# An attention and FFN kernel on one core: all engines in a written order up to the middle of the second FFN group, masks and rescale chains at places of their own, three more filler matmuls

## The chip, the cores and the metric

The kernel runs on one core of a Trainium2 chip. The metric is the device time of one execution in microseconds; the times given are medians over several executions of the same program. A core has five engines with an instruction queue each: TensorE (PE in the profile, its weight loads PEld), VectorE (DVE), ScalarE (ACT), GpSimd (POOL) and SyncE (SP). Each works through its own queue in order. An instruction can wait for semaphores that other engines or DMA transfers raise; everything behind it on the same engine then waits too.

## The reference

Sliding-window attention with four sink tokens feeds a gated FFN:

```python
keep = is_sink | in_window                     # window 128, first 4 tokens always kept
a = softmax(where(keep, q @ k.T / sqrt(64), -1e9))
x = (a @ v)                                    # (4, 8, 768, 64) -> (3072, 512)
xn = x / sqrt(mean(x * x) + 1e-6) * rms_g
out = (silu(xn @ w_gate) * (xn @ w_val)) @ w_out
```

q, k and v are 4 batches x 8 heads x 768 tokens x 64; w_gate and w_val are 512 x 1536, w_out is 1536 x 512. Inputs and output are float32. The kernel works in bfloat16 with float32 accumulation.

## The kernel before

The 3072 tokens are 24 blocks of 128 (`g` = 0 to 23, 6 a batch). Block `g` goes through these units:

- `unit_load` (L126): POOL issues three DMAs, q, k and v of the block (L108, L121), converted to bfloat16 on the way.
- `unit_t` and `unit_t1` (L284, L265): q and k are transposed on TensorE (L260) into PSUM (`pqk`) and copied to `qkT` by DVE or ACT (L298, L274). From block 12 on SP does it by DMA (L290).
- `unit_s` (L431): scores of the block's keys against the queries of the block and of the next one (L443, `pT`), exponential on ACT (L452, `et`), and the masks. `mask` (L411) takes DVE, one multiplication for all heads of a half (L418), for blocks below `POOL_MASK_FROM` and for the first block of a batch, and otherwise two `affine_select` for each half on POOL (L420, L425).
- `unit_attend` (L511): sink part (L476) and values (L490, L494) into `pv`; DVE divides by the sums (L526 `rden`, L531 `x`); ACT sums the squares (L548 `sq`).
- `unit_rms` (L560), the rescale chain: some six tiny DVE instructions (L565 to L593, `m` and `y`) find one over the root; `unit_xr` (L600) multiplies the block by it and by the gain (L611, `xr`).
- `unit_x` (L631): `xr` is transposed on TensorE (L638, `pxt`) and copied to `xnt` (L650, L652); from block 12 on by DMA.
- Four blocks make one FFN group (`G` = 0 to 5). `parts_f` (L671): gate matmuls (L664, `pg`), tanh on ACT (L682, `th`), value matmuls (L664, `pvl`), and two products on DVE (L687 `p`, L697 `hT`). `parts_o` (L741): output matmuls (L748, `po`), eviction on ACT (L755, `osb`), store by SP (L759).

All PSUM tiles come from one pool of eight banks, so a TensorE instruction that opens a tile also waits until ACT or DVE has read the tile that held its bank before.

`run` (L783) writes the order: it walks over the FFN parts of a group and puts the attention units of later blocks between them, each at the part number given beside it in a list. For some engines this order is binding (`manual_schedule`); on the others a planner orders the instructions by its own estimates. Before, all five engines are bound in the opening (L797) and in `byhand` (L851), the first half of group 0. From `first` on (L901) only TensorE, SP and POOL are bound; DVE and ACT are left to the planner. There the masks of a block are issued together with its scores, the chain of blocks 5, 6 and 7 hangs on the end of `unit_av` (L506), and the sink tiles of batch 1 (`unit_sink`, L334) are held behind a tanh. `unit_warm` (L355) multiplies a tile of zeros and nobody reads the result; the opening has six of these matmuls at its start and one later on.

The stretch around the change: blocks 4 to 7 are attended while group 0 ends and group 1 begins. Group 1 works in two column halves, of which the second, from part 12 on, is the one that needs blocks 6 and 7.

Of the kernel before, what the change touches and what calls it, by code (L numbers as in the profile page):

```python
# [28 lines left out]
def kernel(  # L29
# [26 lines left out]
    GB = 4  # L56
# [10 lines left out]
    DMA_X_FROM = 12  # L67
    LD = 15
    FA = FTN
    POOL_MASK_FROM = 8  # L70
    MANUAL = {mybir.EngineType.PE, mybir.EngineType.SP, mybir.EngineType.Pool}
    MANUAL_ALL = MANUAL | {mybir.EngineType.Activation, mybir.EngineType.DVE}

# [258 lines left out]
        VSK[b] = vs  # L332

    def unit_sink(b):  # L334
        with tc.issue_after(LAST_TANH[0]):
            unit_sink_k(b)
            unit_sink_v(b)
# [93 lines left out]
    def unit_s(g):  # L431

        b, t = divmod(g, NT)
        nq = 2 if t + 1 < NT else 1
        w = nq * P
        per = 512 // w
        nb = HP // per
        banks = [[bank() for hi in range(2)] for u in range(nb)]
        for hp in range(HP):
            u, j = divmod(hp, per)  # L440
            for hi in range(2):
                pr = slice(hi * D, (hi + 1) * D)
                nc.tensor.matmul(  # L443
                    out=banks[u][hi][:, j * w:(j + 1) * w],
                    lhsT=QKT[b][pr, 1, hp, t * P:(t + 1) * P],
                    rhs=QKT[b][pr, 0, hp, t * P:t * P + w],
                    start=True, stop=True,
                )
        for u in range(nb):
            et = epool.tile([P, 2, per, nq, P], BF16, name="et")  # L450
            for hi in range(2):
                nc.scalar.activation(  # L452
                    out=et[:, hi].rearrange("p j n c -> p (j n c)"), in_=banks[u][hi],
                    func=ACT.Exp, scale=inv_sqrt_d,
                )

            def masked(u, et, his):
                for hi in his:
                    for j in range(per):
                        for n in range(nq):  # L460
                            E[(g, 2 * (u * per + j) + hi, n)] = et[:, hi, j, n, :]
                e = et if len(his) == 2 else et[:, his[0]:his[0] + 1]
                mask(e.rearrange("p i j n c -> p (i j) n c"), g, nq)

            for his in [(0, 1)] if nq == 2 else [(0,), (1,)]:
                masked(u, et, his)

    PVB = {}

    def unit_sink_av(g):  # L470
        b, t = divmod(g, NT)
# [10 lines left out]
    def unit_av(g, u):  # L482
        b, t = divmod(g, NT)

        pv = PVB.pop((g, u)) if t >= 2 else psum.tile(
            [P, 512], FP32, name="pv", tag="b1")
        for i, h in enumerate(range(H)[heads_of(g, u)]):
            dest = pv[:, i * VW:(i + 1) * VW]
            if t >= 1:
                nc.tensor.matmul(  # L490
                    out=dest, lhsT=E[(g - 1, h, 1)], rhs=V16[b][:, t - 1, h, :],
                    start=(t == 1), stop=False, skip_group_check=True,
                )
            nc.tensor.matmul(  # L494
                out=dest, lhsT=E[(g, h, 0)], rhs=V16[b][:, t, h, :],
                start=(t == 0), stop=True, skip_group_check=True,
            )
        if u == 0:
            X16[g] = xpool.tile([P, H, D], BF16, name="x16", bufs=7)
        pvv = pv[:, 0:HW].rearrange("p (h c) -> p h c", c=VW)  # L500
        if g < 2:
            PV[(g, u)] = pvv
        else:
            unit_norm(g, u, pvv)
            unit_sq(g, u)
        if u == 1 and g in (5, 6, 7):  # L506
            unit_rms(GROUP[g])
            for i in GROUP[g]:
                unit_xr(i)

    def unit_attend(g):  # L511

# [87 lines left out]
    def unit_xr(g):  # L600
        y = Y.pop(g)
        x16 = X16.pop(g).rearrange("p h d -> p (h d)")
        xr = xpool.tile([P, DM], BF16, name="xr", bufs=4)
        if g == 1:
            nc.scalar.mul(xr, x16, y)
        elif g == 0:
            nc.vector.tensor_scalar(
                out=xr, in0=x16, scalar1=y, scalar2=None, op0=ALU.mult,
            )
        else:  # L610
            nc.vector.scalar_tensor_tensor(  # L611
                out=xr, in0=x16, scalar=y, in1=gb, op0=ALU.mult, op1=ALU.mult,
            )
        G, tb = divmod(g, GB)
        if tb == 0:
            XNT[G] = xtpool.tile([P, KTN, GN], BF16, name="xnt")
        if g >= DMA_X_FROM:
            nc.sync.dma_start_transpose(  # L618
                out=XNT[G][:, :, tb * P:(tb + 1) * P], in_=xr,
            )  # L620
        else:
            XR[g] = xr
# [155 lines left out]
                slots[4].append(lambda n=n: unit_t(n))  # L778
        return [(p + i, u) for i, us in enumerate(slots) for u in us]

    AT = [(10, 16, 20, 24, 30), (0, 10, 18, 27)]

    def run(parts, slots):  # L783

# [12 lines left out]
    with tc.manual_schedule(engines=MANUAL_ALL):  # L797
# [8 lines left out]
        unit_t1(1, 0)  # L806
        unit_sp(0, 0)
        unit_t1(1, 1)
        unit_sp(0, 1)
        unit_sp(1, 0)  # L810
        unit_sink_k(0)
        unit_attend01(0, 0)
        unit_attend01(0, 1)
# [29 lines left out]
    def fa(ft, **kw):  # L843
        return parts_f(0, (ft, ft + 1), h0, **kw)
# [1 line left out]
    def fq(cols, ft):  # L846
        return parts_f(0, tuple(range(ft, ft + 4)), cols)

    byhand = (fa(0, split=True, between=lambda: (unit_rms((2,)), unit_xr(2))) + fa(2) + fa(4) + fq(b2, 0) + fa(6) + fq(b2, 4) + fa(8))
    first = fa(10) + fq(b3, 0) + fq(b3, 4) + fq(b2, 8) + fq(b3, 8)  # L850
    with tc.manual_schedule(engines=MANUAL_ALL):  # L851
        run(byhand, [
            (1, lambda: unit_sink_v(0)),
            (1, lambda: unit_sink_scores(0, 2, 1)),
            (2, lambda: unit_attend(2)),
            (7, lambda: unit_x(2)),
            (7, lambda: unit_t1(3, 0)),
            (7, lambda: unit_bias(2, 1)),
            (8, lambda: unit_t1(3, 1)),
            (9, lambda: unit_sink_scores(0, 3, 1)),  # L860
            (9, lambda: unit_sp(2, 1)),
            (9, lambda: unit_bias(3, 0)),
            (9, lambda: unit_sp(3, 0)),
            (11, lambda: unit_attend(3)),
            (12, lambda: (unit_rms((3,)), unit_xr(3))),
        ])
    FIRST = [
        (2, lambda: unit_x(3)),
        (1, lambda: unit_t1(4, 0)),
        (1, lambda: unit_bias(3, 1)),  # L870
        (2, lambda: unit_t1(4, 1)),
        (2, lambda: unit_sp(3, 1)),
        (2, lambda: unit_t1(5, 0)),
        (4, lambda: unit_sink_scores(0, 4)),
        (4, lambda: unit_s(4)),
        (5, lambda: unit_t1(5, 1)),
        (6, lambda: unit_s(5)),
        (7, lambda: unit_t(6)),
        (8, lambda: unit_attend(4)),
        (10, lambda: unit_attend(5)),  # L880
        (16, lambda: unit_t(7)),
        (16, lambda: unit_sink(1)),
        (18, lambda: unit_s(6)),
        (18, lambda: unit_x(4)),
        (19, lambda: unit_x(5)),
        (19, lambda: unit_t(8)),
        (21, lambda: unit_attend(6)),
        (22, lambda: unit_s(7)),
        (24, lambda: unit_t(12)),
        (24, lambda: unit_t(13)),  # L890
# [2 lines left out]
        (0, lambda: unit_t(9)),  # L893
        (4, lambda: unit_attend(7)),
        (4, lambda: unit_x(6)),
        (6, lambda: unit_sink_scores(1, 2)),
        (6, lambda: unit_s(8)),
        (7, lambda: unit_t(10)),
        (9, lambda: unit_x(7)),
    ]  # L900
    with tc.manual_schedule(engines=MANUAL):  # L901

        for g in range(2 * GB + 2, 2 * GB + 6):
            FIRST.append((3 * g - 30, lambda g=g: unit_load(g)))
        for G in range(NG):
            if G == 0:
                parts, slots = first, FIRST
            else:
                parts, slots = [], []
                for cols in (h0, h1) if G == 1 else (slice(0, GN),):  # L910
                    n = GN // (cols.stop - cols.start)
                    for ft in range(0, FTN, n):
                        parts += parts_f(G, tuple(range(ft, ft + n)), cols)
                g0, n = (9, 5) if G == 1 else (4 * G + 6, 4)
                for g in range(g0, min(g0 + n, NB + 1)):
                    slots += step(g, AT[G > 1][g - g0])
                if G == 1:
                    slots += SECOND
                    for g, p in enumerate((0, 0, 7, 11, 17, 21, 25, 27, 31, 33), 14):
                        slots.append((p + 0.5, lambda g=g: unit_load(g)))  # L920
                if G + 2 <= NG:
                    gs = GROUP[GB * (G + 1)]
                    slots.append((25, lambda gs=gs: unit_scale(gs)))
                    for i, g in enumerate(gs):
                        slots.append((30 + i, lambda g=g: unit_x(g)))
            for tb in range(GB):
                parts += (parts_last if G * GB + tb == NB - 1 else parts_o)(G, tb)
            run(parts, slots)
# [1 line left out]
_INS = ['q', 'k', 'v', 'n_sink', 'window', 'moe_w_gate', 'moe_w_val', 'moe_w_out', 'moe_rms_g']  # L930
_OUTS = [((3072, 512), 'float32')]
# [30 lines left out]
```

## Time and profile before

| | |
|---|---|
| median of 7 runs | 249.03 us (248.65 to 250.43) |
| the profiled execution | 248.56 us, of which its span 246.9 us |
| TensorE busy | 238.8 us, 97% of the span |
| DVE busy | 165.4 us, 67% |
| ACT busy | 137.9 us, 56% |
| POOL busy | 104.2 us, 42% |
| granted TensorE clock | 1.00 of full in the profiled execution |

The span runs from the first to the last instruction of the program. Busy shares are means over stages with different limits. A row of a timeline gives start and duration in us, engine, line, operation, what is written and read, how many instructions of a kind follow each other, and in brackets how long the engine had been idle and who ended that. A row of the waits reads: who waited for whom, us in total, how often, the longest. Matmuls are pipelined, so a row's duration is longer than the distance to the next one's start.

### The profile page before, as it was taken

How to read it: one execution, taken by the hardware profiler on the slowest of the kernel's cores; microseconds unless marked ns; L12 is line 12 of the kernel's file. 1: busy time of each engine (PE TensorE's matmuls, PEld its weight loads, DVE VectorE, ACT ScalarE, POOL GpSimd, SP SyncE). 2: the span in 40 equal slices, each digit the busy share in tenths (PEclk: the TensorE clock that was granted, in tenths of full speed). 3: DMA queues.
4: the chain of work that ended last, by engine and by line, in shares of the span. 5: the costliest groups of instructions: out<-in, count | busy, mean ns of one | idle time of the engine just before them, and what ended most of it. 6: DMA issues, size and time to landing. Idle time of an engine off the chain costs nothing.

```text
span 246.9 us, 5312 instructions
## 1 busy us (share of the span) xinstructions
PE 238.8 (97%) x2022; PEld 138.2 (56%) x2041; DVE 165.4 (67%) x379; ACT 137.9 (56%) x323; POOL 104.2 (42%) x141
## 2 busy tenths in 40 slices
PE   8999999999979999999999999999999999999995
PEld 3668788756867884554454444444444444344443
DVE  5648788756998688349778278769168885097700
ACT  3795669446566875975583385674465242323212
POOL 8976677498868598871232001233131000000000
PEclk9999999999999999999999999999999999999999
DMA  9999999999999999999001665001610004710012
GB/s 129 144 183 179 193 157 207 166 176 187 203 149 135 72 84 141 160 187 158 0 0 24 169 170 69 1 0 25 191 42 3 0 0 45 171 42 0 1 73 101
DMA packets 104940, 25.52 MB, mean 103 GB/s; under 512 B 94033, under 2 KB 101969, under 8 KB 104914
## 3 DMA queue, kind: packets, MB, share of 16 engines
q0 software_dynamic: 80704, 13.90, 77.6%
q1 hardware_dynamic: 23026, 10.95, 20.4%
q10 hardware_dynamic: 1184, 0.33, 0.6%
q8 instruction: 16, 0.26, 0.4%
q14 instruction: 10, 0.08, 0.1%
HBM read 28.31 MB, written 6.29 MB: 140 GB/s over the span
## 4 chain that ended last, share of the span: by engine, by line
PE 83%; DVE 12%; issue 1%; SPq 1%; DMA 1%; ACT 1%; DVEq 0%; ACTq 0%
PE pg L664 23%; PE pvl L664 22%; PE po L748 19%; PE pT L443 3%; PE pv L490 3%; PE pv L494 2%; DVE xr L611 2%; PE pqk L260 2%; DVE p L687 2%; DVE hT L697 2%; PE pT L370 1%; SPq L618 1%; PE pw L359 1%; DVE x L531 1%; PE po L730 1%
## 5 line engine op out<-in xcount | busy, mean ns | idle before, releaser
L664 PE MATMUL pg<-xnt,wg 128*128 128x512 bf16 (+2 forms) x431 | 74.0, 304 | 1.4 <-DMA xnt<-xr 0.5
L664 PE MATMUL pvl<-xnt,wv 128*128 128x512 bf16 (+2 forms) x438 | 74.2, 305 | 0.1
L687 DVE SCALAR_TENSOR_TENSOR p<-th,pg 128x512 bf16<-128x512 bf16 x72 | 49.1, 684 | 27.8 <-ACT th L682 27.7
L682 ACT ACTIVATE th<-pg 128x512 bf16<-128x512 f32 x72 | 43.0, 601 | 38.6 <-PE pg L664 37.0
L748 PE MATMUL po<-wo,hT 128*128 128x512 bf16 x268 | 61.4, 379 | 0.4
L697 DVE TENSOR_TENSOR hT<-p,pvl 128x512 bf16<-128x512 bf16 x72 | 49.4, 687 | 7.6 <-DVE p L687 0.5
L664 PEld LDWEIGHTS <-wv 128*128 128x128 bf16 x440 | 38.6, 98 | 24.4
L664 PEld LDWEIGHTS <-wg 128*128 128x128 bf16 x440 | 37.1, 98 | 23.8 <-issue 1.7
L420 POOL TENSOR_SCALAR_AFFINE_SELECT et<-et 128x512 bf16<-128x512 bf16 x28 | 18.8, 677 | 69.9 <-ACT et L452 67.8
L748 PEld LDWEIGHTS <-hT 128*128 128x128 bf16 x276 | 26.3, 98 | 29.8
L452 ACT ACTIVATE et<-pT 128x512 bf16<-128x512 f32 x72 | 37.3, 605 | 6.7 <-PE pT L443 6.6
L755 ACT ACTIVATE osb<-po 128x512 f32<-128x512 f32 x23 | 13.7, 595 | 33.5 <-PE po L748 26.2
L548 ACT ACTIVATE sq<-x 128x256 bf16<-128x256 bf16 x47 | 19.7, 423 | 16.3 <-DVE x L531 14.8
L121 POOL DMA_DIRECT2D v<-in_v_dram x24 | 21.5, 898 | 4.4 <-DMA wo<-in_moe_w_out_dram 1.8
L108 POOL DMA_DIRECT2D qs<-in_q_dram x23 | 20.8, 906 | 4.9 <-DMA wo<-in_moe_w_out_dram 3.1
L108 POOL DMA_DIRECT2D ks<-in_k_dram x23 | 20.6, 895 | 3.0 <-DMA wg<-in_moe_w_gate_dram 1.5
L526 DVE RECIPROCAL rden<-pv 128x4 f32<-128x4 f32 x48 | 7.6, 172 | 20.1 <-PE pv L494 20.1
L531 DVE TENSOR_TENSOR x<-pv,rden 128x256 bf16<-128x256 f32 x48 | 19.7, 422 | 0.9
L611 DVE SCALAR_TENSOR_TENSOR xr<-x,y,gb 128x512 bf16<-128x512 bf16 x22 | 17.2, 830 | 0.3
L425 POOL TENSOR_SCALAR_AFFINE_SELECT et<-et 128x512 bf16<-128x512 bf16 x22 | 14.4, 656 | 0.0
L494 PE MATMUL pv<-v,et 128*128 128x65 bf16 x160 | 11.8, 194 | 0.0
L443 PE MATMUL pT<-qkT 64*128 64x256 bf16 (+1 forms) x160 | 11.6, 261 | 0.0
(86 smaller groups left out, 189.5 us busy)
## 6 DMA issues: line engine op xcount, KB each, us to landing
out_dram<-osb SPq DMA_DIRECT2D x21, 256.0 KB, 2.4
v<-in_v_dram POOLq DMA_DIRECT2D x24, 128.0 KB, 7.7
qs<-in_q_dram POOLq DMA_DIRECT2D x23, 128.0 KB, 7.3
ks<-in_k_dram POOLq DMA_DIRECT2D x23, 128.0 KB, 7.0
wg<-in_moe_w_gate_dram POOLq DMA_DIRECT2D x6, 256.0 KB, 8.7
wv<-in_moe_w_val_dram POOLq DMA_DIRECT2D x6, 256.0 KB, 9.0
wo<-in_moe_w_out_dram POOLq DMA_DIRECT2D x2, 768.0 KB, 11.0
out_dram<-osb SPq DMA_DIRECT2D x4, 128.0 KB, 2.3
```

Of the source, the lines that this page charges most:

```text
L108: nc.gpsimd.dma_start(out=tl, in_=src[b, :, t * P:(t + 1) * P, :].rearrange("h t d -> t h d"),)
L121: nc.gpsimd.dma_start(out=V16[b][:, t, :, 0:D], in_=v[b, :, t * P:(t + 1) * P, :].rearrange("h t d -> t h d"),)
L443: nc.tensor.matmul(out=banks[u][hi][:, j * w:(j + 1) * w], lhsT=QKT[b][pr, 1, hp, t * P:(t + 1) * P], rhs=QKT[b][pr, 0, hp, t * P:t * P + ...
L452: nc.scalar.activation(out=et[:, hi].rearrange("p j n c -> p (j n c)"), in_=banks[u][hi], func=ACT.Exp, scale=inv_sqrt_d,)
L531: nc.vector.tensor_tensor(out=X16[g][:, heads_of(g, u), :], in0=pvv[:, :, 0:D], in1=RDEN.pop((g, u)).unsqueeze(2).to_broadcast((P, 4, D)), ...
L548: nc.scalar.activation(out=sq, in_=xh, func=ACT.Square, scale=MS_SCALE, accum_out=MS[g - i][:, i, u:u + 1],)
L611: nc.vector.scalar_tensor_tensor(out=xr, in0=x16, scalar=y, in1=gb, op0=ALU.mult, op1=ALU.mult,)
L664: nc.tensor.matmul(out=ps[:, i * w + c0:i * w + c0 + n], lhsT=w_sb[:, kt, ft * P:(ft + 1) * P], rhs=XNT[G][:, kt, cols], start=(kt == 0), ...
L682: LAST_TANH[0] = nc.scalar.activation(out=st["th"], in_=st["pg"], func=ACT.Tanh, scale=0.5).ins
L687: nc.vector.scalar_tensor_tensor(out=p1, in0=st["th"], scalar=1.0, in1=st["pg"], op0=ALU.add, op1=ALU.mult,)
L697: LAST[0] = nc.vector.tensor_tensor(out=HT[key][:, i:i + n, cols], in0=p1.rearrange("p (n c) -> p n c", n=n), in1=st["pvl"].rearrange("p ( ...
L748: nc.tensor.matmul(out=st["po"], lhsT=HT[(G, ft // 4)][:, ft % 4, tb * P:(tb + 1) * P], rhs=wo[:, ft, :], start=(ft == 0), stop=(ft == FTN ...
```

## The change

Five edits:

1. `POOL_MASK_FROM` goes from 8 to 7: block 7's masks move from DVE to POOL.
2. Masks of the blocks below that number are no longer issued with their scores but by `unit_m`, at a place of its own in the list (blocks 4, 5 and 6). The rescale chains become `unit_chain`, with a place of their own (blocks 2 to 7).
3. DVE and ACT are bound to the written order also for the rest of group 0 and for the first 12 parts of group 1 (`N1`). After that they are left to the planner as before. `unit_sink(1)` is no longer held behind a tanh.
4. Some units move: block 5's transposes from slot 19 to 20 of group 0; in group 1 block 10's from 7 to 5, scores of 8 from 6 to 7, scores of 9 and values of 8 to fixed places, block 7's transposes from 9 to 11.
5. One filler matmul ahead of block 0's second scores, and two ahead of block 0's values.

```diff
-    POOL_MASK_FROM = 8
+    POOL_MASK_FROM = 7
...
     def unit_sink(b):
+        if b == 1:
+            unit_sink_k(b)
+            unit_sink_v(b)
+            return
...
             for his in [(0, 1)] if nq == 2 else [(0,), (1,)]:
-                masked(u, et, his)
+                f = lambda u=u, et=et, his=his: masked(u, et, his)
+                MASKS.setdefault(g, []).append(f) if g < POOL_MASK_FROM else f()
+
+    def unit_m(g):
+        for f in MASKS.pop(g):
+            f()
...
-        if u == 1 and g in (5, 6, 7):
-            unit_rms(GROUP[g])
-            for i in GROUP[g]:
-                unit_xr(i)
+
+    def unit_chain(*gs):
+        unit_rms(gs)
+        for g in gs:
+            unit_xr(g)
...
-    AT = [(10, 16, 20, 24, 30), (0, 10, 18, 27)]
+    AT = [(16, 20, 24, 30), (0, 10, 18, 27)]
...
         unit_t1(1, 1)
+        unit_warm(1)
         unit_sp(0, 1)
         unit_sp(1, 0)
+        unit_warm(2)
         unit_sink_k(0)
         unit_attend01(0, 0)
...
     FIRST = [
...
+        (6, lambda: unit_m(4)),
         (6, lambda: unit_s(5)),
         (7, lambda: unit_t(6)),
+        (8, lambda: unit_m(5)),
         (8, lambda: unit_attend(4)),
         (10, lambda: unit_attend(5)),
+        (11, lambda: unit_chain(4, 5)),
         (16, lambda: unit_t(7)),
         (16, lambda: unit_sink(1)),
         (18, lambda: unit_s(6)),
         (18, lambda: unit_x(4)),
-        (19, lambda: unit_x(5)),
+        (19, lambda: unit_m(6)),
         (19, lambda: unit_t(8)),
+        (20, lambda: unit_x(5)),
         (21, lambda: unit_attend(6)),
+        (22, lambda: unit_chain(6)),
         (22, lambda: unit_s(7)),
...
         (0, lambda: unit_t(9)),
         (4, lambda: unit_attend(7)),
         (4, lambda: unit_x(6)),
+        (5, lambda: unit_t(10)),
+        (5, lambda: unit_chain(7)),
         (6, lambda: unit_sink_scores(1, 2)),
-        (6, lambda: unit_s(8)),
-        (7, lambda: unit_t(10)),
-        (9, lambda: unit_x(7)),
+        (7, lambda: unit_s(8)),
+        (10, lambda: unit_s(9)),
+        (11, lambda: unit_x(7)),
+        (11, lambda: unit_attend(8)),
+        (14, lambda: unit_t(11)),
     ]
...
+    N1 = 12
     with tc.manual_schedule(engines=MANUAL):
...
+        parts, slots = group(1)
+        with tc.manual_schedule(engines=MANUAL_ALL - MANUAL):
+            run(byhand, BYHAND)
+            run(first + outs(0), FIRST)
+            run(parts[:N1], [e for e in slots if e[0] < N1])
+        run(parts[N1:], [(p - N1, f) for p, f in slots if p >= N1])
+        for G in range(2, NG):
+            run(*group(G))
```

`group(G)` builds a group's parts and slots as the loop did before.

More of the change, by code (lines that the diff above doesn't have):

```diff
@@ L465, in unit_s @@
             for his in [(0, 1)] if nq == 2 else [(0,), (1,)]:
-                masked(u, et, his)
-    PVB = {}
+                f = lambda u=u, et=et, his=his: masked(u, et, his)
[3 more added lines that the diff above has]
+            f()
+    MASKS, PVB = {}, {}
     def unit_sink_av(g):
@@ L847, in fq @@
         return parts_f(0, tuple(range(ft, ft + 4)), cols)
-    byhand = (fa(0, split=True, between=lambda: (unit_rms((2,)), unit_xr(2))) + fa(2) + fa(4) + fq(b2, 0) + fa(6) + fq(b2, 4) + fa(8))
+    byhand = (fa(0, split=True, between=lambda: (unit_chain(2),)) + fa(2) + fa(4) + fq(b2, 0) + fa(6) + fq(b2, 4) + fa(8))
     first = fa(10) + fq(b3, 0) + fq(b3, 4) + fq(b2, 8) + fq(b3, 8)
[L851 to L866, printed above, removed]
+    BYHAND = [
+        (1, lambda: unit_sink_v(0)),
+        (1, lambda: unit_sink_scores(0, 2, 1)),
+        (2, lambda: unit_attend(2)),
+        (7, lambda: unit_x(2)),
+        (7, lambda: unit_t1(3, 0)),
+        (7, lambda: unit_bias(2, 1)),
+        (8, lambda: unit_t1(3, 1)),
+        (9, lambda: unit_sink_scores(0, 3, 1)),
+        (9, lambda: unit_sp(2, 1)),
+        (9, lambda: unit_bias(3, 0)),
+        (9, lambda: unit_sp(3, 0)),
+        (11, lambda: unit_attend(3)),
+        (12, lambda: unit_chain(3)),
+    ]
     FIRST = [
-        (2, lambda: unit_x(3)),
         (1, lambda: unit_t1(4, 0)),
         (1, lambda: unit_bias(3, 1)),
+        (2, lambda: unit_x(3)),
         (2, lambda: unit_t1(4, 1)),
@@ L895 @@
         (4, lambda: unit_x(6)),
+        (5, lambda: unit_t(10)),
+        (5, lambda: unit_chain(7)),
         (6, lambda: unit_sink_scores(1, 2)),
-        (6, lambda: unit_s(8)),
-        (7, lambda: unit_t(10)),
-        (9, lambda: unit_x(7)),
-    ]
-    with tc.manual_schedule(engines=MANUAL):
[L903 to L928, printed above, removed]
@@ new lines, with group @@
+        (7, lambda: unit_s(8)),
[3 more added lines that the diff above has]
+        (14, lambda: unit_t(11)),
+    ]
+    for g in range(2 * GB + 2, 2 * GB + 6):
+        FIRST.append((3 * g - 30, lambda g=g: unit_load(g)))
+    def group(G):
+        parts, slots = [], []
+        for cols in (h0, h1) if G == 1 else (slice(0, GN),):
+            n = GN // (cols.stop - cols.start)
+            for ft in range(0, FTN, n):
+                parts += parts_f(G, tuple(range(ft, ft + n)), cols)
+        g0, n = (10, 4) if G == 1 else (4 * G + 6, 4)
+        for g in range(g0, min(g0 + n, NB + 1)):
+            slots += step(g, AT[G > 1][g - g0])
+        if G == 1:
+            slots += SECOND
+            for g, p in enumerate((0, 0, 7, 11, 17, 21, 25, 27, 31, 33), 14):
+                slots.append((p + 0.5, lambda g=g: unit_load(g)))
+        if G + 2 <= NG:
+            gs = GROUP[GB * (G + 1)]
+            slots.append((25, lambda gs=gs: unit_scale(gs)))
+            for i, g in enumerate(gs):
+                slots.append((30 + i, lambda g=g: unit_x(g)))
+        return parts + outs(G), slots
@@ new lines, in outs @@
+    def outs(G):
+        parts = []
+        for tb in range(GB):
+            parts += (parts_last if G * GB + tb == NB - 1 else parts_o)(G, tb)
+        return parts
+    N1 = 12
+    with tc.manual_schedule(engines=MANUAL):
+        parts, slots = group(1)
[6 more added lines that the diff above has]
+            run(*group(G))
```

## The prediction

> **What bounds the kernel now.** I read the page first, then the waits of TensorE alone, then the chain that ended last inside the stretch that the change touches, then the timelines of DVE and POOL there.
>
> ```profile
> span 246.9 us, 5312 instructions
> PE 238.8 (97%) x2022; PEld 138.2 (56%) x2041; DVE 165.4 (67%) x379; ACT 137.9 (56%) x323; POOL 104.2 (42%) x141
> PE 83%; DVE 12%; issue 1%; SPq 1%; DMA 1%; ACT 1%; DVEq 0%; ACTq 0%
> ```
>
> TensorE is busy 97% of the span and carries 83% of the last chain; 12% is DVE. So a gain can only come from a place where TensorE stands still or runs work that it need not. Its waits between 60 and 84 us, the widest hole of the whole run:
>
> ```profile
> PE pxt L638 <- DVE xr L611: 1.4, 1, 1.4
> PE pv L476 <- DVE hT L697: 0.2, 1, 0.2
> ```
>
> Comparing the starts of neighbouring matmuls (a 128x256 matmul starts every 0.109 us, 8 of them in 0.87), I find 0.21 lost at 68.17, 0.11 at 68.50, 1.52 at 73.08, 0.33 at 75.06, 0.22 at 75.40: 2.4 us together. The chain of waits in this stretch is almost all DVE, from block 6's norm at 59.77 to the copy of block 7's transposes at 75.35: DVE is the bound there. Why it is late (DVE's own timeline, start and duration first):
>
> ```profile
> 61.53 0.22 DVE L576 SCALAR_TENSOR_TENSOR y<-y,m 128x1 f32<-128x1 f32 x1
> 61.78 0.16 DVE L585 SCALAR_TENSOR_TENSOR y<-y 128x1 f32<-128x1 f32 x1
> ...
> 62.73 0.74 DVE L611 SCALAR_TENSOR_TENSOR xr<-x,y,gb 128x512 bf16<-128x512 bf16 x1
> 63.38 1.28 DVE L418 TENSOR_TENSOR et<-et,masks 128x1024 bf16<-128x1024 bf16 x2
> ...
> 70.13 0.60 DVE L576 SCALAR_TENSOR_TENSOR y<-y,m 128x1 f32<-128x1 f32 x1
> 70.76 0.55 DVE L585 SCALAR_TENSOR_TENSOR y<-y 128x1 f32<-128x1 f32 x1
> ...
> 71.94 1.08 DVE L611 SCALAR_TENSOR_TENSOR xr<-x,y,gb 128x512 bf16<-128x512 bf16 x1
> ```
>
> The same instructions of a rescale chain take 0.22, 0.16, 0.74 for block 6 and 0.60, 0.55, 1.08 for block 7. Block 7's run beside POOL's four masks of block 8:
>
> ```profile
> 70.09 0.63 POOL L420 TENSOR_SCALAR_AFFINE_SELECT et<-et 128x512 bf16<-128x512 bf16 x1 [2.18 <-DVE y L571]
> 70.68 0.63 POOL L425 TENSOR_SCALAR_AFFINE_SELECT et<-et 128x512 bf16<-128x512 bf16 x1
> 71.26 0.63 POOL L420 TENSOR_SCALAR_AFFINE_SELECT et<-et 128x512 bf16<-128x512 bf16 x1
> 71.85 0.63 POOL L425 TENSOR_SCALAR_AFFINE_SELECT et<-et 128x512 bf16<-128x512 bf16 x1
> ```
>
> L576 ends at 70.73, L420 at 70.72; L585 and L425 both end at 71.31. The excess (0.38+0.39+0.32+0.34) is 1.4 us, and TensorE's long wait is 1.5.
>
> **The change, part by part.** The built order of each engine shows: TensorE gets three filler matmuls and some blocks trade places; DVE loses two L418, POOL gains two L420 and two L425; ACT and SP issue the same instructions, ACT in another order; behind the middle of the second group nothing differs but the 1:1 shift.
>
> *Fillers.* The first stands where TensorE waits for DVE's copy anyway (idle from about 8.20 to 8.56 behind the eight score matmuls that follow it): 0.22 into 0.36, cost 0. The other two stand ahead of block 0's values:
>
> ```profile
> 8.56 0.41 PE L385 MATMUL pT<-qkT 64*128 64x128 bf16 x8 [0.18 <-DVE qkT L274]
> 8.90 0.42 PE L494 MATMUL pv<-v,etp 128*128 128x65 bf16 x8
> 9.25 1.12 PE L194 MATMUL pgb<-osb,gb 1*128 1x512 f32 x2
> 10.30 0.20 PE L490 MATMUL pv<-v,etp 128*128 128x65 bf16 x1
> ```
>
> The last score matmul is issued at 8.78. Two fillers at 0.216 (the warm spacing of 128x512 matmuls: 22 of L748 span 4.91) end at 9.21, so the values start at 9.22 instead of 8.90, and TensorE is then solid (0.35, twice 0.53) up to block 1's values, which move from 10.30 to 10.63. From those hang the norm, the squares, the first rescale and the first FFN matmul at 15.45. Cost 0.33; ends 0 (if 8.90 waits for something else as well) and 0.45.
> [...] The row: loads of the same idle weights take 0.15 at 2.31 and 0.10 at 12.59, and from 6.4 on transposes start every 0.056; the longest hole from there to 15.5 is 0.5 us. [...] by this row they save nothing and cost 0.33. I take the row; two of the seven runs are 1.4 above the others, without anything that shows why, so a lower end of -0.2 remains.
>
> *Tail of the first group (38 to 57 us).* On DVE block 4's two masks (0.6 each) go behind one product pair (p then hT, 1.38 from start to start), block 5's behind the next, and block 4's norm behind both. Laid out with those durations: masks of 4 end at 43.8 and 44.5, needed by the values at 44.30 and 44.54; masks of 5 end at 46.5, needed at 46.93; block 4's norm ends at 47.59 instead of 46.31, so ACT's squares and the tanh behind them end at 48.6 instead of 47.39, and the last product pair and block 5's norm at 51.2. Squares (51.8), chain (1.25), two xr (1.42), copy of block 7's q and k (0.68) end at 55.1 instead of 53.9. The scores that need it started at 55.10. Cost 0.05, between 0 and 0.4: the cover is used up. ACT's two evictions there start at 51.8 and 52.8; their banks are wanted at 55.1 and later, and the copy of ksk, now behind them, some 13 us later.
>
> *Block 7's masks to POOL.* DVE saves 1.2 (two L418 at 0.6). POOL gets four of 0.63, started every 0.59, when the exps are there: 62.9 and 64.0 for the two halves, the needed L420 ends 63.5 and 64.6. The values want them at 64.9 and 65.2: 0.6 spare. Behind them in POOL's queue the loads of blocks 14 and 15 move from 61.52 to 65.3; block 14's transposes on SP (issued at 70.14 in the trace) go to some 74, their users come behind 96: free. POOL's masks of block 8 wait for ACT, not for these loads.
> [...] If the new masks met block 6's chain as those of block 8 met block 7's, 1.4 would come back. By the layout that chain has started its xr at 62.45, ahead of 62.9: only 0.3 to 0.6 of one instruction is exposed, and DVE then waits for a tanh until 64.43 anyway. [...] I take no collision.
>
> *Block 7's chain, scores 8, transposes 10 and 7 (61 to 83 us).* DVE from 64.43: two product pairs (2.76), norm of 7 (1.09), copy of block 6's transposes (0.34), copy of block 10 (0.61), chain (1.11, undisturbed), xr (0.65) end at 71.0. Block 8's masks start at 71.3, since ACT now runs two squares, tanh, sink exp and tanh first. So the collision is gone, and the xr is there 3 us before its transposes, which stand two parts later. TensorE with its waits: scores 8 wait 0.15 for the copy of block 10, the next pvl 0.25 for the bank of the sink exp (69.80), small ones 0.05, the values of 8 wait 0.3 for a product (DVE's third pair ends its p at 74.43), the values of 9 0.18. By the values of 9 both kernels have done the same work: 82.54 before, 80.80 after. Gain 1.74; ends 2.7 (all of these waits gone; DVE gives back 1.2+1.4) and 0.7 (a second collision, or 1 us more of waits).
>
> *Sum.* -1.74+0.05(counted in it)+0.33 = -1.4. Span 246.9 to 245.5; the profiled execution took 248.56, 1.66 more than its span, so 247.2; the median of the runs shown is 0.47 above that: 247.6 us.
>
> **The rivals.** *The waits only change their name* (A): in the stretch DVE stays the bound, and the tanh behind the squares holds TensorE's banks. For it: DVE is laid solid from 64.4 to 75.2, with 0.3 between xr and block 8's masks; against it: 2.6 us of DVE time really go. It gives -0.7+0.45 or so: 248.8.
> *The first group's tail comes late* (B, slower): place, DVE's copy of block 7's q and k ahead of scores 6, laid out for 55.1 against a need at 55.10. The path to it, from block 4's masks over values, norm, squares, tanh, products, norm, squares and chain, changes engine nine times, and no slack is left; each us late is a us of TensorE, and everything behind shifts with it. It eats the forecast's 1.4 from 1.4 us late, and is measurable as a loss from 2.7; at 2.8 (0.3 more at each handover than the 0.04 to 0.10 that the trace shows there) 250.4. For it: nine steps in series laid out from durations alone; against it: the old order had 1.2 us of slack here with the same instructions, and each of their durations is in the trace.
> *Everything clears* (C): all of TensorE's 2.4 and the odd tenths go, and the fillers cost nothing: 246.5.
> *The change does nothing* would need the order to be the old one; the built order differs, so this has no chance of its own.
>
> **How the numbers follow.** Forecast 0.62 (own range 246.9 to 248.3), A 0.17, B 0.13, C 0.08. Half a per cent, about what this kernel's measurement can tell from no change, is 1.25 us: faster means below 247.8. Of the forecast three quarters lie there, and all of C: 0.54. Slower (above 250.3): B, 0.13. Same: the rest of the forecast and A, 0.33. The range leaves out B and the far half of C: 246.6 to 249.3.
>
> **What would show it.** Right: L576, L585, L593 of block 7 near 0.2, its xr near 0.7; no wait of pxt for xr; a p or esk named in short waits between 68 and 75; L494 of block 1 at 10.6, first FFN matmul near 15.8. Wrong: scores 6 waiting over 0.4 for the copy L298 near 55; values of 7 waiting for POOL's L420; y rows of 0.5 in block 6's or 7's chain; a first FFN matmul at 15.5 or earlier.

## The result, and the profile after

The changed kernel takes 247.31 us (median of 12 runs, 246.69 to 248.56); the kernel before, run beside it, 248.94 us. The ratio is 0.9929, with a 95% interval from 0.9911 to 0.9948: faster by 0.7%. The forecast was 247.6 us, range 246.6 to 249.3. The profiled execution has a span of 245.3 us (before 246.9), and the forecast for it was 245.5.

The page of the kernel after, busy times, granted clock and the chain that ended last:

```profile
span 245.3 us, 5321 instructions
PE 239.0 (97%) x2025; PEld 138.1 (56%) x2044; DVE 163.9 (67%) x377; ACT 138.5 (56%) x323; POOL 107.3 (44%) x145
PEclk9999999999999999999999999999999999999999
PE 80%; DMA 6%; DVE 6%; POOL 4%; issue 1%; SPq 1%; ACT 1%; DVEq 0%; ACTq 0%; POOLq 0%
```

DVE's share of the last chain fell from 12% to 6%; DMA's rose from 1% to 6%. TensorE's waits in the kernel after (who waited for whom, total, times, longest):

```profile
PE pw L363 <- DVE idle L99: 1.1, 1, 1.1
PE pss L348 <- DMA qkT<-qs: 0.5, 1, 0.5
PE pg L674 <- DVE xnt L655: 0.2, 1, 0.2
PE pg L674 <- DMA xnt<-xr: 0.2, 1, 0.2
PE pxt L648 <- DVE xr L617: 0.2, 1, 0.2
```

The wait of 1.4 for block 7's `xr` is gone. A new one has come, later in the run: 0.5 for a DMA transpose (`pss` is the tile of the sink scores). DVE's timeline around block 7's chain, first the two rows of the kernel before that the prediction does not show, then the kernel after:

```profile
71.24 0.15 DVE L589 SCALAR_TENSOR_TENSOR y<-y 128x1 f32<-128x1 f32 x1
71.42 0.48 DVE L593 SCALAR_TENSOR_TENSOR y<-y 128x1 f32<-128x1 f32 x1
```

and

```profile
69.49 0.22 DVE L586 SCALAR_TENSOR_TENSOR y<-y,m 128x1 f32<-128x1 f32 x1
69.74 0.16 DVE L595 SCALAR_TENSOR_TENSOR y<-y 128x1 f32<-128x1 f32 x1
69.82 0.15 DVE L599 SCALAR_TENSOR_TENSOR y<-y 128x1 f32<-128x1 f32 x1
70.00 0.16 DVE L603 SCALAR_TENSOR_TENSOR y<-y 128x1 f32<-128x1 f32 x1
70.20 0.75 DVE L621 SCALAR_TENSOR_TENSOR xr<-x,y,gb 128x512 bf16<-128x512 bf16 x1
```

The first and the last of POOL's four masks of block 8 in the kernel after:

```profile
71.16 0.63 POOL L424 TENSOR_SCALAR_AFFINE_SELECT et<-et 128x512 bf16<-128x512 bf16 x1 [0.45 <-ACT et L456]
...
72.92 0.63 POOL L429 TENSOR_SCALAR_AFFINE_SELECT et<-et 128x512 bf16<-128x512 bf16 x1
```

The chain that took 0.60, 0.55, 0.15, 0.48 and 1.08 before takes 0.22, 0.16, 0.15, 0.16 and 0.75, because it is over at 70.95 and POOL's masks start at 71.16.

**Where the time came from.** The opening (up to the first FFN matmul) differs from one execution to the next by more than a us, as shown below. So the profiles are compared by stages: *stage* is the time from the first FFN matmul to the first matmul for block 9's values, and *rest* is what follows it. Between these two starts the two profiles have the same 810 matmuls of TensorE, in another order. The two ends of the stage, before and after:

```profile
15.45 0.61 PE L664 MATMUL pg<-xnt,wg 128*128 128x128 bf16 x8 [0.18 <-DVE xnt L645]
82.54 0.28 PE L476 MATMUL pv<-vsk,esk 64*128 64x260 bf16 x2
```

and

```profile
15.42 0.61 PE L674 MATMUL pg<-xnt,wg 128*128 128x128 bf16 x8 [0.18 <-DVE xnt L655]
80.75 0.27 PE L485 MATMUL pv<-vsk,esk 64*128 64x260 bf16 x2
```

The first three columns of the table are from one profiled execution each. "Places" are the part numbers in the lists. A median is over all executions of a kernel; a ratio leaves out those more than 1.5% above the fastest (one of the 22 with three places, one of before beside it).

| kernel | first FFN matmul | stage | rest | median | ratio to before, 95% |
|---|---|---|---|---|---|
| before | 15.45 | 67.09 | 164.3 | 248.94 | |
| after | 15.42 | 65.33 | 164.5 | 247.31 | 0.9929 [0.9911, 0.9948] |
| after, a second time | 16.23 | 65.32 | 164.2 | 247.16 | 0.9911 [0.9878, 0.9945] |
| after without fillers | 16.03 | 65.33 | 164.2 | 247.87 | 0.9932 [0.9906, 0.9958] |
| after, chain of 7 one product pair later | 16.76 | 67.08 | 164.5 | 249.59 | 1.0015 [0.9994, 1.0036] |
| after, masks of 7 on DVE | 16.78 | 65.88 | 163.7 | 247.90 | 0.9931 [0.9908, 0.9954] |
| before with the fillers | 16.88 | 67.11 | 163.9 | 249.01 | 0.9995 [0.9971, 1.0019] |
| before with masks of 7 on POOL | 16.01 | 68.65 | 164.1 | 250.38 | 1.0037 [1.0020, 1.0055] |
| before with three places | 16.01 | 65.95 | 164.1 | 247.75 | 0.9948 [0.9928, 0.9969] |
| after, planner from group 1 on | 15.35 | 65.26 | 164.0 | 247.27 | 0.9916 [0.9886, 0.9945] |
| after, planner from `first` on | 16.33 | 64.89 | 164.5 | 247.30 | 0.9920 [0.9897, 0.9943] |
| after, transposes of 15 early | 15.41 | 65.32 | 163.8 | 246.43 | 0.9904 [0.9866, 0.9941] |
| the same, a second time | 16.90 | 65.32 | 164.2 | 247.65 | 0.9927 [0.9899, 0.9954] |
| the same without fillers | 16.01 | 65.32 | 164.3 | 247.04 | 0.9913 [0.9893, 0.9932] |

The six profiles that share the change's order in the stage agree to 0.01 us (65.32 to 65.33), while their openings lie 1.5 us apart. The change gained 1.76 in the stage.

### The profile page after: what moved, and what is told of

Read it like the earlier page. It is cut to its first block, busy times and chain, and to the rows that moved or that the text cites. A ratio compares the mean times of both kernels' runs of the same rounds, so it can differ in the third digit from the quotient of the medians.

```text
span 245.3 us, 5321 instructions
## 1 busy us (share of the span) xinstructions
PE 239.0 (97%) x2025; PEld 138.1 (56%) x2044; DVE 163.9 (67%) x377; ACT 138.5 (56%) x323; POOL 107.3 (44%) x145
## 4 chain that ended last, share of the span: by engine, by line
PE 80%; DMA 6%; DVE 6%; POOL 4%; issue 1%; SPq 1%; ACT 1%; DVEq 0%; ACTq 0%; POOLq 0%
PE pg L674 24%; PE pvl L674 23%; PE po L758 16%; DMA qkT<-qs 3%; PE pT L447 3%; PE pv L499 2%; PE pqk L260 2%; PE pv L503 2%; DMA ks<-in_k_dram 1%; DVE xr L621 1%; PE pw L363 1%; PE pT L374 1%; PE po L740 1%; SPq L628 1%; POOL qs L108 1%
## 5 line engine op out<-in xcount | busy, mean ns | idle before, releaser
L424 POOL TENSOR_SCALAR_AFFINE_SELECT et<-et 128x512 bf16<-128x512 bf16 x30 | 20.7, 694 | 67.0 <-ACT et L456 67.0
L429 POOL TENSOR_SCALAR_AFFINE_SELECT et<-et 128x512 bf16<-128x512 bf16 x24 | 15.8, 659 | 0.0
```

Of the source, the lines that this page charges most:

```text
L424: nc.gpsimd.affine_select(out=ev[:, :, 0, :], in_=ev[:, :, 0, :], compare_op=ALU.is_ge, fill=0.0, base=0, pattern=[[0, x], [1, P]], channe ...
```

## The experiments

### The yardstick, and the change without its fillers

The changed kernel ran again unchanged:

> The changed kernel once more, beside the three variants of it, so that they have their own yardstick: 247.3 us, 0.993 of before. First pair of scores near 6.9 or 7.3 us: theory 'the granted clock rises at another moment in each execution' expects it to differ from run to run by some tenths, with the first FFN matmul between 15.4 and 15.8; theory 'the order does it' expects 6.87 and 15.42 again.

247.16. The first scores stood at 7.64 instead of 6.87 and the first FFN matmul at 16.23 instead of 15.42, with the same program. That speaks for the theory of the clock (the four transposes at 6.62 took 0.50 us here and the four behind them 0.39; the profile of after, which records full clock from 4.88 on, has 0.38 for the four at 6.37), but 16.23 lies beyond the 15.8 that it allowed for.

```diff
-        unit_warm(1)
         unit_sp(0, 1)
         unit_sp(1, 0)
-        unit_warm(2)
```

> The changed kernel without its three filler matmuls (their products are read by nobody). Theory 'fillers cost 0.33, an earlier clock hid it in the one profile': block 0's values 0.3 earlier, near 8.6 at the clock of the profile of after, the first FFN matmul near 15.1, time 247.0. Rival 'block 0's values wait for something else, the fillers lie in a hole': values at 8.9, first FFN matmul 15.4, time unchanged at 247.3. Rival 'the fillers make the clock rise earlier': scores at 7.3, first FFN matmul 15.45 or later, time 247.3 to 247.7.

Between the first scores and block 0's values lie 1.60 us (2.04 with fillers), so the local cost of the fillers is 0.44. The time did not get shorter: 247.87 in place of 247.16, with overlapping intervals. No theory met its numbers. The first FFN matmul stood at 16.03, because DVE's `xr` of block 0, which now started at 14.01, took 0.71 instead of 0.35 to 0.39 (more on this row in the last section).

### One swap on DVE

```diff
-        (5, lambda: unit_chain(7)),
+        (6, lambda: unit_chain(7)),
         (6, lambda: unit_sink_scores(1, 2)),
```

Only DVE's order differs: one product pair stands ahead of the chain instead of behind it.

> One swap on DVE alone: block 7's rescale chain behind the next product pair instead of ahead of it; all other engines keep their order, and DVE has the same instructions. [...] the chain then falls beside POOL's masks of block 8 (71.2 to 73.5), its y rows take 0.5 to 0.6 instead of 0.16 to 0.22 and its xr 1.1 instead of 0.75, DVE is 1.2 to 1.5 later behind it, and the values of block 8 wait that much for a product: 248.5 to 248.8. Rival 'it was the lead of xr and the DVE sum, not the coincidence': xr ends near 73.1, still ahead of its transposes at 74.0, the product for block 8's values ends where it did (74.3), 247.3.

DVE's timeline in this kernel:

```profile
72.50 0.64 DVE L586 SCALAR_TENSOR_TENSOR y<-y,m 128x1 f32<-128x1 f32 x1
73.17 0.55 DVE L595 SCALAR_TENSOR_TENSOR y<-y 128x1 f32<-128x1 f32 x1
73.65 0.15 DVE L599 SCALAR_TENSOR_TENSOR y<-y 128x1 f32<-128x1 f32 x1
73.83 0.48 DVE L603 SCALAR_TENSOR_TENSOR y<-y 128x1 f32<-128x1 f32 x1
74.35 1.08 DVE L621 SCALAR_TENSOR_TENSOR xr<-x,y,gb 128x512 bf16<-128x512 bf16 x1
```

and POOL's:

```profile
72.49 0.63 POOL L424 TENSOR_SCALAR_AFFINE_SELECT et<-et 128x512 bf16<-128x512 bf16 x1 [0.44 <-DVE y L581]
73.08 0.63 POOL L429 TENSOR_SCALAR_AFFINE_SELECT et<-et 128x512 bf16<-128x512 bf16 x1
73.67 0.63 POOL L424 TENSOR_SCALAR_AFFINE_SELECT et<-et 128x512 bf16<-128x512 bf16 x1
```

These are the durations of before (0.60, 0.55, 0.15, 0.48, 1.08) again, but for 0.04 in the first. TensorE's longest wait in this kernel is not for `xr`, but for the product behind the chain, which has to free a PSUM bank:

```profile
PE pg L674 <- DVE p L697: 1.7, 1, 1.7
```

The stage is 67.08, that of before to 0.01. So the coincidence with the masks costs the time, by making the products behind the chain late; the lead of `xr` does not matter here. It was dearer than expected (1.75 in the stage for 1.2 to 1.5): besides the stretch of 1.46, DVE waited 0.19 for the tanh of the pair that was moved ahead. The median, 249.59, is 0.8 above the range expected. It also holds more of the lower clock described in the last section: 14 of the 22 executions have a granted clock of 0.993 or less, against 1 of 6 in the second run of after.

### The parts one at a time

The masks of block 7 back to DVE, the rest of the change kept:

```diff
-    POOL_MASK_FROM = 7
+    POOL_MASK_FROM = 8
...
+        (1, lambda: unit_m(7)),
```

> The changed kernel with block 7's masks left on DVE (two of 0.6, ahead of the second group's first product). Theory 'the masks' 1.2 us of DVE are half of the gain': every product behind them 1.2 later, block 7's chain at 70.3 and its xr inside POOL's masks of block 8 (some 0.35 more), the values of block 8 wait 1.3 to 1.6 for a product: 248.6 to 248.9, the gain all but gone. Rival 'the order carries the gain, DVE's sum has slack': below 247.8.

247.90, stage 65.88: this costs 0.55, which is between the theory and its rival. Everything on DVE is 1.2 later, but TensorE then waits 0.42 inside block 8's scores, for the copy of block 10's transposes, and 0.21 behind them, for a sink exponential. So the masks of 8 come later too (73.16, where the chain's `xr` ends at 72.95), there is no collision, and the late products fall into slack.

The masks on POOL, in the kernel before, nothing else:

```diff
-    POOL_MASK_FROM = 8
+    POOL_MASK_FROM = 7
```

> The kernel before with block 7's masks on POOL, no other edit. From the first FFN matmul to the values of block 9 before took 67.09 us and the changed kernel 65.33. Theory 'the masks' 1.2 us on DVE pull block 7's chain ahead of POOL's masks of block 8, so most of the 1.44 of stretch goes with them': y rows 0.16 to 0.22, at most xr stretched, TensorE's wait for xr 0.2 or less, 65.5 to 65.9, time 247.4 to 247.8, most of the gain without the order. Rival 'only the written order takes the chain out of the masks': y rows still 0.5, 66.5 or more, 248.4 or more.

The theory falls and the rival's bounds are met: 250.38, stage 68.65, slower than before by 0.4% (0.2% to 0.55%). DVE's timeline in this kernel:

```profile
70.39 0.22 DVE L576 SCALAR_TENSOR_TENSOR y<-y,m 128x1 f32<-128x1 f32 x1
70.65 0.48 DVE L585 SCALAR_TENSOR_TENSOR y<-y 128x1 f32<-128x1 f32 x1
71.06 0.15 DVE L589 SCALAR_TENSOR_TENSOR y<-y 128x1 f32<-128x1 f32 x1
71.24 1.85 DVE L593 SCALAR_TENSOR_TENSOR y<-y 128x1 f32<-128x1 f32 x1
73.12 1.08 DVE L611 SCALAR_TENSOR_TENSOR xr<-x,y,gb 128x512 bf16<-128x512 bf16 x1
```

POOL's masks of block 8 in the same kernel:

```profile
71.21 0.69 POOL L420 TENSOR_SCALAR_AFFINE_SELECT et<-et 128x512 bf16<-128x512 bf16 x1
71.80 0.69 POOL L425 TENSOR_SCALAR_AFFINE_SELECT et<-et 128x512 bf16<-128x512 bf16 x1
72.39 0.68 POOL L420 TENSOR_SCALAR_AFFINE_SELECT et<-et 128x512 bf16<-128x512 bf16 x1
72.97 0.67 POOL L425 TENSOR_SCALAR_AFFINE_SELECT et<-et 128x512 bf16<-128x512 bf16 x1
```

One y row of a single column took 1.85 us: it started 0.03 after the first mask and ended at 73.09, with the third. The planner had put a product between the chain's first two instructions, so the chain was early by only 0.3, and met the masks at its end. (The 0.48 of L585 ends at 71.13, ahead of the first mask; what lengthened it is not shown.) TensorE stood 2.3 us and then, by the table of stretches of this kernel, ran on a lower clock. The columns are the stretch, its length, the busy us of PE, PEld, DVE, ACT and POOL with their instructions, the granted clock, the DMA share and GB/s:

```profile
72.00:74.00 2.00, 0.00 (x0) 0.00 (x0) 1.97 (x2) 0.60 (x1) 2.00 (x4) 1.00 2.44 155
74.00:76.00 2.00, 1.74 (x18) 1.22 (x20) 1.90 (x4) 0.00 (x0) 2.00 (x3) 0.82 2.00 173
76.00:78.00 2.00, 2.00 (x26) 1.35 (x23) 1.90 (x5) 1.77 (x4) 0.84 (x3) 0.50 2.27 174
78.00:80.00 2.00, 2.00 (x17) 1.66 (x16) 0.98 (x5) 1.47 (x5) 2.00 (x5) 0.83 1.20 81
```

From the values of block 8 to those of block 9 it took 8.25 us where before took 7.48, so 0.77 was lost behind the hole as well.

Three places alone, in the kernel before:

```diff
-        (6, lambda: unit_s(8)),
-        (7, lambda: unit_t(10)),
-        (9, lambda: unit_x(7)),
+        (5, lambda: unit_t(10)),
+        (7, lambda: unit_s(8)),
+        (11, lambda: unit_x(7)),
```

> The kernel before with three places of the second group alone: transposes of block 10 at part 5 instead of 7, scores of block 8 at 7 instead of 6, transposes of block 7's x at 11 instead of 9 (masks of 7 stay on DVE, DVE's and ACT's order stays with the scheduler). First FFN matmul to values of block 9: before 67.09, all places with the masks on DVE 65.88, the change 65.33. Theory 'these places carry most of it: POOL's masks of block 8 come 1 us later and xr is asked for two parts later': 65.9 to 66.5, time 247.9 to 248.5. Rival 'block 7's chain, cut up by the scheduler, then falls beside the masks of 8 as before': 66.8 or more, 248.7 or more.

247.75, stage 65.95: the stage lies in the theory's range, at its good end, and the median 0.15 below the range. The masks of 8 on POOL start at 71.42, so only the last y row (0.48) and `xr` (1.08) are stretched. The wait moves to the values of block 8, and is this kernel's largest in the stage:

```profile
PE pv L476 <- DVE hT L697: 0.8, 1, 0.8
```

### Is the written order of DVE and ACT needed?

```diff
-    N1 = 12
+    N1 = 0
```

> The changed kernel with DVE and ACT left to the scheduler from the second group on (masks of 7 on POOL and all places as in the change, TensorE and POOL in the same order): on DVE block 7's chain is then cut up between two product pairs. Theory 'the chain has to stand in one piece ahead of the masks': its last y and its xr fall beside the masks of block 8 (0.48 to 0.55, and 1.08), the product for block 8's values is about 0.8 later, first FFN matmul to values of block 9 66.0 to 66.5 where the change has 65.33, time 247.9 to 248.3. Rival 'places and masks are enough': 65.3 to 65.5, 247.2.

247.27, stage 65.26: the theory falls. The planner does cut the chain up, the last y takes 0.27 and `xr` 1.08, but its order puts a product ahead of the chain's end, and the product for block 8's values is in time.

The same for all that follows `byhand` (the block of DVE and ACT bindings ends there):

> The changed kernel with DVE and ACT left to the scheduler from the tenth part of the first FFN on, as in the kernel before; the places, the masks on POOL and the fillers stay. Theory 'places and masks carry the gain, the written order of DVE and ACT nothing': first FFN matmul to scores of block 6 39.75 to 39.85 and to values of block 9 65.2 to 65.5, time 247.0 to 247.5. Rival 'the written order is needed in the first group': scores of block 6 waiting 0.3 or more, 247.8 or more.

(The expectations call the planner the scheduler.) 247.30, stage 64.89, which is 0.44 *better* than the written order, though block 7's last y takes 0.40 and its `xr` 1.08 beside the masks here too. Block 6's values come 43.67 after the first FFN matmul, as before (43.68); in the change it is 43.80. So the written order of DVE and ACT, the third of the five edits, brings nothing that these runs can show, and costs 0.12 in the tail of the first group.

### Fillers alone, and the late transpose

```diff
+        unit_warm(1)
         unit_sp(0, 1)
         unit_sp(1, 0)
+        unit_warm(2)
```

> The kernel before with the three filler matmuls alone. From the first scores to block 0's values before took 1.59 us, the changed kernel 2.04. Theory 'fillers cost 0.4 up to block 1's values, and keep TensorE's clock up': 2.04 here too, first scores to first FFN matmul 8.5 to 8.6 where before has 8.14, but fewer runs in the upper cluster (before: 7 of 35 runs at 250.0 or more): median 249.0 to 249.4. Rival 'the fillers help the median': below 248.8. Rival 'they cost nothing': 248.9 to 249.1 with the same share above 250.

From the first scores to block 0's values it took 2.04, as expected. The first FFN matmul came 9.32 behind the first scores, and not 8.5 to 8.6, in an execution with a mean granted clock of 0.993. The median, 249.01, cannot be told from that of before beside it, 249.12. No execution of this kernel is above 249.97 and five of before are above 250.2, but with 14 executions that decides nothing.

The new wait in the profile of after is this row of TensorE's timeline:

```profile
103.79 0.29 PE L348 MATMUL pss<-qkT,ksk 128*32 128x256 bf16 x4 [0.50 <-DMA qkT<-qs]
```

and these of SP's queue:

```profile
94.80 0.35 SPq L769 DMA_DIRECT2D out_dram<-osb  x1
95.24 1.29 SPq L290 DMA_TRANSPOSE qkT<-qs  x1
```

Block 15's transposes stand behind a store. They were moved eight parts ahead:

```diff
-            if n < NB and n not in (10, 12, 13) and by_dma(n) == (n == g + 3):
+            if n < NB and n not in (10, 12, 13, 15) and by_dma(n) == (n == g + 3):
...
+        (20, lambda: unit_t(15)),
```

> The changed kernel with the DMA transposes of block 15 issued eight parts earlier on SP (ahead of the second group's stores). In one profile of the change the sink scores of blocks 14 and 15 waited 0.66 for them at 103.79, in another, whose prologue was 0.8 later, not at all. Theory 'the DMA queue is a floor that takes back the gain where the prologue is quick': transposes land 1.5 us or more before the sink scores, no wait there, runs with a quick prologue 0.45 faster, the others the same: median 246.9 to 247.2, lowest run 246.4. Rival 'the transposes only push other transfers back': a wait of 0.3 or more elsewhere, 247.2 to 247.6.

> The change with block 15's DMA transposes issued early, a second time, as yardstick for the variant without fillers: 246.4 to 247.1, below the change's 247.2 to 247.3 by 0.1 to 0.5 if a late transfer is what the change loses in some runs; 247.2 or more if the first reading was luck.

The wait is gone in both profiles, but the medians are 246.43 and 247.65, on both sides of the change. So the first reading was luck, and the theory of a floor is not shown: the lowest executions (246.14 and 246.30) lie below those of the change (246.69 and 246.96), but with the old place and the planner's order from group 1 on one took 246.09. In the profiles of before and of the nine experiments with the old place, this transpose takes 6.8 to 8.2 us from issue to landing, whatever the opening was; in the profile of after it took 8.5, where some 7.9 would have been in time (TensorE lost 0.66 here, of which the row has 0.50 in its bracket). With the planner's order from `first` on it was late once more, by 0.18. So it is a wait of single executions.

> The same without the three filler matmuls (their products are read by nobody). Profiles with fillers have 2.04 from first scores to block 0's values, those without 1.59. Theory 'the fillers cost 0.4 and give nothing': 0.3 to 0.45 below the version with fillers. Rival 'they give back what they cost, by the granted clock': within 0.2 of it, or slower, with more runs 1.3 above the lowest.

247.04 (246.64 to 247.33), half-way between the two readings of the same kernel with fillers. None of these three can be told from the change.

## Why the prediction was right

In short: the mechanism forecast for the stretch from 61 to 83 us is in the main the one that the runs show, and it carries the gain. The term for the fillers was not borne out, and that the sum came so close is luck in part.

*Fillers.* 0.33 was forecast, with ends 0 and 0.45. At its place the cost is there, at the upper end: 2.04 in place of 1.59 from the first scores to block 0's values. In the time nothing of it can be found (0.9995 for the fillers alone), and in the profile of after block 1's values stand at 10.30 and the first FFN matmul at 15.42. The second of these the prediction had named as a sign of being wrong. The openings scatter: full clock is recorded from 4.88 us on in the profile of after and from 6.20 in that of before, and after's scores were 0.44 earlier. I let one row decide, but the first FFN matmuls of the profiles lie up to 1.5 us apart (15.35 to 16.90), which one profile of before could not show. That the fillers keep the clock up is not shown either: the two openings in which a table of stretches has a lower clock (0.53 from 12 to 15 us with the swapped chain, 0.61 with the masks of 7 on DVE) are of kernels with fillers. Nor were the two runs that puzzled the prediction without a sign: in the later rounds each of the 12 executions of before between 250.2 and 251.1 has a granted clock of 0.986. For the two runs themselves no clock is on record.

*Tail of the first group.* Forecast: copy of block 7's transposes at 55.1, scores of 6 just behind it, cost 0.05. Measured: 55.12, scores at 55.18, block 6's values 0.12 later against the first FFN matmul than before. That is right, and the planner's order has no such cost. Rival B did not happen.

*Masks on POOL.* No collision with block 6's chain was forecast. The chain kept its durations. The first mask started at 62.87 beside `xr` and took 0.85 instead of 0.63, so some 0.3 of the 0.6 spare was left, and the values of 7 did not wait. The loads of blocks 14 and 15 moved behind the masks as laid out, to 65.44.

*Stretch 61 to 83.* Gain 1.74 forecast for the values of 9, 1.76 measured in the stage; `xr` to end at 71.0, measured 70.95; masks of 8 from 71.3, measured 71.16; the product `p` for block 8's values to end at 74.43, measured 74.32. The waits that it lists for TensorE add up to 0.93, though (0.15, 0.25, 0.05, 0.3, 0.18), while its own 1.74 and the 0.05 of the tail leave room for 0.60 of the 2.39 lost before; in the profile some 0.5 are left (from block 6's values to block 9's it takes 21.53 us, where before took 23.41). So the closeness of 1.74 to 1.76 is luck in part.

What the prediction did not separate is which part of the change does it. It added 1.2 (masks) and 1.4 (collision). Of the 1.76 in the stage the three places alone bring 1.14; the masks on top of the change's other parts bring 0.55; the masks without the places cost 1.56. Nor does the chain have to be undisturbed: in the planner's order its end is stretched, and yet the stage is as short or shorter (65.26 and 64.89). What counts is whether TensorE waits for something that stands behind the stretch. A collision of masks and chain was weighed for block 6 and passed over; the place where it came is block 7's chain in the old places, as the run with the masks alone shows (stage 68.65, one y row of 1.85).

*Sum.* Span 245.5 forecast, 245.3 measured; median 247.6 against 247.31. The agreement of the spans holds two errors that cancel: the fillers' 0.33 is not in the profile, and the wait of 0.66 at 103.79 was not foreseen, since the built order downstream is the same. In the profile of before this transpose landed at 104.46 for a use at 105.02, half a us to spare; the prediction left out that its duration differs by more than that from one execution to the next (7.7 us to landing in this profile, 8.5 in that of after).

## What to carry to other kernels

When a small serial chain on DVE and a run of masks on POOL feed the same deadline, look at their coincidence before their sums, and at what stands behind the chain: one swap in DVE's queue, with the same instructions, was worth the whole change here (stage 67.08 against 65.33). Move a piece of work to the other engine only together with the places around it; the same edit alone was a loss here (stage 68.65 against 67.09). And where openings scatter, compare stages between two fixed instructions: these agreed to 0.01 us while whole spans differed by 1.8.

## What the runs showed of the hardware

- **DVE's small rows took longer beside POOL's masks.** A y row of 0.16 to 0.22 took 0.48 to 0.64 beside one mask (before, and the swapped chain) and 1.85 beside three masks back to back (masks of 7 on POOL alone). In other places the mask took longer: with the planner's order from group 1 on, two masks beside an `xr` took 1.08 and 1.10 instead of 0.63. The products `p` and `hT` kept their 0.67 to 0.69 beside the same masks.
- **The granted clock differed between executions of one program, and between openings.** Executions of before list means of 0.986 to 1.000. Full clock is recorded from 4.88 us on in the profile of after and from 6.20 in that of before. The tables of stretches give 0.53 from 12 to 15 us and 0.90 from 15 to 18 with the swapped chain, 0.61 and 0.82 with the masks of 7 on DVE, and 1.00 in both stretches for the two profiles of after. The page of the kernel with the swapped chain has it in the third slice:

```profile
PEclk9979999999999999999999999999999999999999
```

  In these two the first FFN matmul stood at 16.76 and 16.78. Two more profiles in which it stood late, at 16.88 (before with the fillers) and 16.90 (transposes of 15 early, a second time), have a mean clock of 0.993; the profiles with fillers and a mean clock of 1.000 have it at 15.35 to 16.33. All four have the fillers, but that the fillers bring on the lower clock is not shown: clocks of 0.993 or less are listed for 4 of 9 executions of after without fillers and for 41 of 99 of before, for 6 of 12 of after and for 5 of 14 of before with the fillers. Where in the execution the lower clock lies is not listed.
- **One hole in TensorE's work was followed by a lower clock.** With the masks of 7 on POOL alone TensorE stood 2.3 us; the three stretches of 2 us from 74 us on have a granted clock of 0.82, 0.50 and 0.83, and another 0.77 was lost. Holes of 1.5 (before) and 1.9 (swapped chain) were not followed by it: the clock is 1.00 in all stretches from 62 to 80 us there. It was no single profile: 20 of the 22 executions of the kernel with the masks alone have a clock of 0.993 or less, against 16 of 37 of before beside it.
- **DVE's `xr` of block 0 took longer beside POOL's issue of a load.** It took 0.35 in the profiles of before and after. In the six profiles in which it started between 13.81 and 14.17 it took 0.53 to 0.89 and ended at 14.70 to 14.73, just behind the end of POOL's issue of block 3's k (13.60 to 14.61). In a seventh the issue was later (13.88 to 14.75), and `xr`, begun at 14.24, ended at 14.84. In the four profiles in which it began less than 0.1 into the issue, or ahead of it, it kept its 0.35. That hides a shorter opening: of the five profiles without fillers four have an `xr` of 0.53 to 0.89, and whether it started at 13.81 or at 14.17, their first FFN matmul stands at 16.01 to 16.03.
